# A ninth tile off ScalarE in six row pairs, and the second pair's x queued earlier, in a striped-window attention kernel

## The chip, the cores and the metric

The kernel runs on one core of one Trainium2 chip. The metric is the device time of one execution in microseconds. A measurement of a kernel is the median of several executions; one further execution is taken with the profiler on, and its trace gives the durations.

## The reference

The input x is one image of 224 × 224 positions with 96 channels, in bf16. Queries, keys and values come from one projection. The first 48 channels attend within horizontal stripes of 8 rows, the other 48 within vertical stripes of 8 columns; each stripe has 8 × 224 = 1792 tokens, and there are 28 stripes of each kind. The two halves are joined and projected.

```python
qkv = jnp.einsum('bhwc,cd->bhwd', x, wqkv)
q, k, v = (qkv[..., :C].copy(), qkv[..., C:2 * C].copy(), qkv[..., 2 * C:].copy())
scale = C2 ** (-0.5)
qh = q[..., :C2].reshape(B * nh, sw * W, C2)
...
ah = _softmax(jnp.einsum('bqc,bkc->bqk', qh, kh) * scale, axis=-1)
oh = jnp.einsum('bqk,bkc->bqc', ah, vh).reshape(B, H, W, C2)
...
av = _softmax(jnp.einsum('bqc,bkc->bqk', qv, kv) * scale, axis=-1)
ov = jnp.einsum('bqk,bkc->bqc', av, vv).reshape(B, nw, H, sw, C2)
...
return jnp.einsum('bhwc,cd->bhwd', o, wo)
```

## The kernel before

**Tiles.** The work goes by 28 pairs of stripes: P = 0 to 13 are the row pairs (horizontal stripes), P = 14 to 27 the column pairs. The two stripes of a pair lie in the two halves of the partitions. The 1792 queries of a pair are cut into four chunks of 512, 512, 512 and 256 columns, its keys into 14 tiles of 128. A tile, as the text uses the word, is one key tile against one chunk of queries for both stripes: 128 × 1024 scores (in the last chunk, two key tiles share one). A pair has 14 + 14 + 14 + 7 = 49 tiles.

**Three ways to the exponential.** Most tiles (kind A, letter `q` in the orders below) are scored by TensorE into one of two sets of PSUM banks (`qk_fn`, L642) and exponentiated by ScalarE (`emit_qk`, L812). The others avoid ScalarE: they are scored twice into banks of a ring of four (`s_fn`, L655), and VectorE and GpSimd work out the exponential by a polynomial in 16-bit numbers. Letter `1` is the first scoring, from which VectorE makes `qb` in two halves ("p1", L852). In kind P, GpSimd then runs three operations on the whole tile (L864, L867, L868). In kind R, VectorE makes a second step from the same banks ("p2", L854, two halves) and GpSimd only squares (L866). Letter `2` is the second scoring, from whose banks VectorE finishes the tile in two halves ("f", L857). `KINDS` (L22) says which of a chunk's last tiles are off ScalarE, chunk by chunk: `"PPR PPR PP "` means three, three, two and none, so eight in a pair (six P, two R) and 41 on ScalarE. `KIND_OF` (L44) picks an entry of `KINDS` for each pair; all have the same one.

**The rest of the work.** Letter `v` multiplies a finished tile with the values (`emit_pv`, L668) into an accumulating bank, which VectorE copies out at the end of a chunk (L829). Letter `k` is a fill for the next pair: its keys, a small correction by the mean key (a product of four columns, L492), its queries and values (L465, L510), each evicted by VectorE. Letter `f` is a fill that projects a finished part of the output with wo (L546 in the row stage, L582 in the column stage), again with its eviction by VectorE (L553 and L561; L589 and L594).

**The order.** The program of each engine is written out by a planner in the kernel's own Python code. `ORDER` (L45) has a string for each pair that says in which order TensorE issues its work; a loop over its letters calls `do_q`, `do_s`, `do_v` and `do_fill`. Assumed durations decide in which order VectorE and GpSimd take what becomes ready, and which bank is used. The eleven tiles after the first are scored twice over (`NTWICE`). `x_t`, fed by `XR1` and `XR2`, is the planner's assumption of when a pair's x is in place; it holds nothing back on the chip, where semaphores do.

**x on its way.** For row pairs from the second on, SP's queue, which is in order, moves x in steps: `block_x(P)` copies two stripes inside DRAM to another layout, `load_x(P)` loads them to `x_sb`, and `turn_x(P)` transposes them by DMA into `xT_sb[P % 2]`, from which the fills read. `keep_x(P)` stores the transposed x to DRAM for the column stage. At the program's start the queue holds pair 0's x, wqkv, block_x(1), block_x(2), and then the eight issues that bring wo and a one into `woh` and `wov`. Those wait for GpSimd to have cleared `woh` and `wov`. Behind them come load_x(1) and turn_x(1), then what `queue_prep` adds at the first tile of each pair:

```python
if P == 1:
    keep_x(0)
    load_x(2)
    keep_x(1)
    block_x(3)
elif P == 2:
    turn_x(2)
    load_x(3)
    keep_x(2)
    block_x(4)
```

Of the kernel before, what the change touches and what calls it, by code (L numbers as in the profile page):

```python
# [42 lines left out]

KIND_OF = [0, 0, 0, 0, 0, 0, 0, 0, 0, 0, 0, 0, 0, 0, 0, 0, 0, 0, 0, 0, 0, 0, 0, 0, 0, 0, 0, 0]  # L44
ORDER = [  # L45
    "kqkkqkq11qkqqk1qqkqvkqq1vvq1qkvq2vqvkvq1qvvvqkq2qvq2vqkvkqkqv1qkq1kqvvvq2vqv2qvvqkq1vvqkq2vqvkvq1qvvvqvkqkfqvvkqv",
    "2qvvq2vqvv1qvvqvvqvvq1vqvvfqv2qvkqkqvvkqkfqvvq2vqv1qvvq2kq2qvvq1vqvvqvvqkvvqkq1vvq2qkvqfvqv2qkvvqkq1vqfvqv2qkvqvvvq1qv1qvkvq",
    "fqvvfqvq2vqv1qvvvqvvqv1qvvq1qq2vqv1qvvqvvqv2qvvkqv1qkvqvq2vqkvkvqv2qvvvq1qvkfqvkqvkqv2qvvqvkq2vqvffqvqvkqvkkqkfqvvq1vqv2qvvvq1",
    "vqv2qvvqf1qvqvvvqvvq1fqqv1qvvq2vqv1qvvqkvqvfqkvqvkvq2qvq2vfqvvqkvq1kq2fqkqvvvq1qkvvqkq2vfqvvq2vqv2qkqvvkq1qvvvqv1qvqkvvkqff",
    "qvv2qvq1qvfqvvvqvq2vqvvvq2vq1qvqvvq1vqvkqv2qvvvqvkq1vqvfqvvqfvqvvvq1vqkkqvvq2kqv2qvvq2vqfvqkvq2vqvkq1qkvvqvkq1qvkvqvfqkvkvq",  # L50
    "fq1vvqv2qvvq1vqvvqvvvq1qvfqv2qvvq1vqvkq1qvvqvvkqkvq2qvvq1vvqkvq2qkfqvvkq1qvvq2qkvqfkqvvqf2qvvqv2qvvvqkq2vvqvkqfqvffqkvvqvvqk",
    "1qvvqv1qvvvq2qvv1qvvqvqv1qvvvqv1qvvq2vqv1qqvvvq2qfvqvvkq2vqvfqvvq1vqkvqvkq2vqvkvq1kq2qvkqkvvq2qvkvq1qvvvq1qkkqkvqv2qkq1q",
    "vvvqvq2vvq1qvvfqvfqvvvqfvq2vqv1qvvq2vqvkvq1qvvqvvvq2vqkvqkvkqv2qvfqkq1vqkvvq1qkvqvv2qkqkvqv1qvvvq2fqvvvqfvq2vqfvqkfqvvqkvq1vqkvvq2v",
    "qv1qvvvqfvqvvq2qvvvq1qv1qvvqvfqvv2qkvqvfqvkqvkq2vqvvkqf1qvvqvvqvqk1qvkqvvq2vqv2qvkqv1qkvqv2qkqvvqvv1qkqvvqv1qvvkqvfqvkvq2qvv2",
    "qvqvvfqvv1qqfvvqvvqv1qvq2vqkq1qkvvq2qvvqkvvq2fqvvqkvq1vqvkqvvqv2qvvqkvq1vqkvqkqvkq2vvqv2qvvq1vqvkqv1qkvqkqfvq1vvqv2qvvq",
    "2fqvqv1qvvvqvvqvvqf1qvvqv2qvvq1kqvqkvqkvq2qkvvfq1qvvvqfvqkqv2qkvqkvq1vqv1qkqvvfqfqvvfqkfqvvq2vqv2qvvq2vqkvqvvq1vvqkvq1vqvvqk",
    "2qvvq2vqfvq1qvvfqvvqvvq2vqvq2vqvv1qvq1vqv1qvvqkvvqkvqkvqvkq1vvq2qfvqkvq2fqvvfqvvq2vqvkqkvqvkq1vqv2qkvqvkq1vqkvqvqv1qfvvqvvkq2",
    "vq1qvqvvq2qvvffqvvq1qvvvqkvvq2qvv2qvqvvkq2vqv1qvkqvffqkvqvq1vkqvvqkvq1vq2qvvvqvfqkvvq2qvvvq1vqkvq2vqvkq2qvkqkvvvq1qkvvvqffqvvkvqf",
    "2qvvqv1qvvfqvvq1qvvvqfvqvvq1q2qvqkv1qvkq2qvvq1vqvkqqvvqvv2qvfqkqvk1q2qvvq2qfvqvkvq2qkvvq1qvv1qkqkvvq1qvkkqvvvq1qkvvvqvvq2v",
    "qvfqvv2qvfqvvq1vqvvq1vqv2qvvqvkq1vqvkvqvvqvkqkvfqv2qvvq2vqvvq2vqvfqkvq1vqkvqvkq2vqvkq1qvv2qvkqvkq1qvvvq1kqvvkqvfqv2qvvq2vqv1qv",  # L60
    "vqfvvqfvqvq1vvqfvqv2qvvqv2qkvqv2qvkqkqvkvq1kq1qvvqkvvqvq1fqvvqvkqvkqkq1vvqkqkv1qvfqq2vvqvq2vqv2qvvvq1vqvvq2vqkvfqvvqffqvvvqv",
    "vq2fqvvvqvqvfqvvv1qvvqqv1qfqvvq2vvqq1vvq2qkvkqkqv2qkvvq1qkvvqvvq2qvvq1fqvvkqvqkvq1vfqvvq2vqkqvv2qvqkkqv2qvvvvq2qvvvkq1qkvvq1vf",
    "qvvfqvvq1qvvvqvvfqvqvkq1qvvvqvkq2qfvvqvq2vvq2qvkvq1qvvvq2vvq1qkvqvkfqqvv2qvvkqq1vvq2qkvvq1qvkfqvkqvvqfqv2vqkvq1vq1qkvqv2qk",
    "vq1qvvvqvvq1qffqvvvqvvqvvq2vq1qvq2vqvkvq1fqvvqvvqv2qvqvkkqvvq1vqvfqkvvqv1qkqfvq2vqvvkqkq2vqvkq2qvkkqvvq2qvv1qvkqvvq1fqvvqk",
    "vfqvv2qvq1qfvqvvqvvqv2qvvqvvkq1qkkqvkqv1qfvqvfqkvq2qvq1vqvvvqv2qvq1vqv1qvvqv2qvvq2vfqvkqvvq2vqvkq1vqkkqvvq2vqkfqkvvqv1qvkvq",
    "2qvvq1vvqvvqvvq1fqvvvqv1qvvqv2qkkqfqvvqfvkqvvq1qkvqvkqv2qvq2vqv1qvkqvvq2vqkvqkq1vqfkqvvvq2qfvvqv2qvvq1vqvvq2vqvkvq2qkvvq1qvvk",
    "fqv2qvq1qvvqvvvq2qvvvq1fqvqfvvqvvqv1qkvqv2qvvqfq2vqvkqkvfqvkqvvq2vqvkq1qkvvqvqv1qvvq1vqkfqkvqfvqkvqkvq2vqkvqvvq1vqv2qvfqk",
    "vvvq1qfvqvvq2vvq2qvv1qvqvvqvvq1vvqkq2vqvv1qvvq2vq1qfqvvvqvkqvkqvkvqv1qkqkq1kq2qvvvq1qkqvv2qkvqfkqkvqvq2vvqv2qvkvqvq1vvq2qv",
    "v1qfqvvvqvvq1vqvfqvvq2vqvvvq1vqv2qvvkqq1vvqvkqvvvq1vqkfqvkqvv2qvvq2qvkvq2qkqk2qvvfqkvqfqvvfqvvvqv1qvkqvfqv1qvvqkvvqkfqvkvvq2qvvvq",
    "2vqvv1qfvqvvvqvq1vvqvvqv1qvq2qkvqkvqfvqv2qvvq1vqv2qvvkqkvfqvqkvq1vqvkqvvqv1qfqv2qvqv1qvq2vfqvvq2vqkqkvvqv1qvq2vqkkvq1qvkqvkv",  # L70
    "q2fqvvvqv1qqvvfqvqvvvq1qvvvq1vqkvqkq1vvqvqvv2qkqkvvq2vqv2qvq1vvqfqk2qvvqkqkkvq2qvvfqvvvq2qvv1qfqvkvqvvq2qvkvvq1qvvvkq1qfvvqfvk",
    "qvfqvq2vvq1qvqvvvq1qvvvqfvq2qvvvq1qvvkqkvq2vqv2qvfqkvqkvvq2vvqvvq2qv1qfqvvvqkqv1qvfqvvvq2qvkqkq1vkqkqvq2vfqvvvq1qvvkvq1qkvk",
    "q2qfvqvq1vqvvvqvqv1qfqvv1qvvqv2qfvvqvq2vvqv2qvq1fqvvqvvvq1vqvqfvvqvv2qfqvvvq2vqfvvq2qvv1qvfqvvfqvvfqv2qvvqffvfqvvq2vqvfqvvvqvqfffvvvvvvfff",
]
# [1126 lines left out]
```

## Time and profile before

| | us |
|---|---|
| median of 3 runs | 1083.1 (1077.69 to 1087.49) |
| profiled execution, its own time | 1083.81 |
| its span, first to last instruction | 1082.0 |
| busy: ScalarE | 1062.8 (98%) |
| busy: TensorE | 1050.6 (97%) |
| busy: VectorE | 1021.5 (94%) |
| busy: GpSimd | 956.4 (88%) |
| mean granted TensorE clock | 0.991 |

The lines of the profile name the engines by short names: PE is TensorE's matmuls and PEld its weight loads, ACT is ScalarE, DVE is VectorE, POOL is GpSimd, SPq is the queue of DMA issues on SyncE. Every row of a group gives the line of the kernel, the engine and operation, the written and read tiles with their shapes, the count, then the busy time and the mean duration of one, and last the idle time of the engine just before these instructions and what ended it. Operations of one engine overlap at their ends, so a mean duration can be longer than the pace. TensorE's busy time says little by itself, since the ends of matmuls are modelled. In a table of stretches each engine has its busy time and, in brackets, its instructions; PEclk is the granted TensorE clock as a share of full speed, and the last two columns are the mean busy share of the DMA engines and the GB/s moved.

### The profile page before, as it was taken

To read this page: it belongs to the slowest core of one execution; us is meant where nothing else is said; L and a number is where in the kernel's file an instruction comes from. 1 tells how busy PE (TensorE), PEld (TensorE's weight loads), DVE (VectorE), ACT (ScalarE), POOL (GpSimd) and SP (SyncE) were. 2 spreads that over 40 slices of the span, in tenths; PEclk is the share of its full clock that TensorE was granted. 3 is DMA by queue.
4 is the path that set the end of the run, shared out by engine and by line. 5 is a ranking of instruction groups with operands and counts; after the bars stand their busy time and mean duration, and the time that the engine had idled before them with its cause. 6 is when DMAs were issued, how large, how long until landed. Compare 5 with 4: busy or idle time off the path is not lost. (4 is left out here: it accounts for less than half of the span.)

```text
span 1082.0 us, 34436 instructions
## 1 busy us (share of the span) xinstructions
PE 1050.6 (97%) x14096; PEld 403.5 (37%) x14096; DVE 1021.5 (94%) x2246; ACT 1062.8 (98%) x1159; POOL 956.4 (88%) x597
## 2 busy tenths in 40 slices
PE   8999999999999999999999999999999999999997
PEld 3333433433333333334333333333433333333333
DVE  7799999999989999999999999999999999999998
ACT  7899999999999999999999999999999999999997
POOL 8979898879998888898999978998997997998895
PEclk9799999999999999999999999999999999999999
DMA  7997426516724650400001022112111110210112
GB/s 147 154 165 112 69 46 112 80 38 108 112 44 71 112 86 2 61 28 27 2 27 32 16 54 48 40 23 50 40 25 43 44 42 18 53 44 18 26 23 39
DMA packets 236994, 61.73 MB, mean 57 GB/s; under 512 B 227780, under 2 KB 234148, under 8 KB 236836
## 3 DMA queue, kind: packets, MB, share of 16 engines
q1 hardware_dynamic: 235716, 59.04, 30.1%
q8 instruction: 110, 1.80, 0.7%
q10 hardware_dynamic: 1120, 0.49, 0.2%
q14 instruction: 48, 0.39, 0.1%
HBM read 28.31 MB, written 28.21 MB: 52 GB/s over the span
## 5 line engine op out<-in xcount | busy, mean ns | idle before, releaser
L812 ACT ACTIVATE PT<-ps 128x1024 bf16<-128x1024 f32 x1148 | 1058.5, 1081 | 9.5 <-PE ps L642 8.2
L642 PE MATMUL ps<-QT_sb,KT_sb 49*64 49x512 bf16 (+1 forms) x5420 | 480.0, 364 | 15.3 <-ACT PT L812 9.7
L668 PE MATMUL ps<-PT,V_sb 128*49 128x512 bf16 (+1 forms) x3136 | 466.3, 364 | 0.1
L864 POOL TENSOR_TENSOR PT<-qb 128x1024 f16<-128x1024 f16 x168 | 316.8, 1894 | 68.1 <-DVE qb L852 45.0
L868 POOL TENSOR_TENSOR PT<-PT,qb 128x1024 f16<-128x1024 f16 x168 | 355.8, 2127 | 8.5
L857 DVE SCALAR_TENSOR_TENSOR PT<-ps,PT 128x512 uint16<-128x512 f32 x448 | 290.5, 683 | 22.7 <-PE ps L655 13.3
L852 DVE TENSOR_SCALAR qb<-ps 128x512 f16<-128x512 int16 x448 | 291.6, 683 | 10.5 <-PE ps L655 7.3
L642 PEld LDWEIGHTS ps<-QT_sb,KT_sb 49*64 49x64 bf16 x5420 | 144.0, 104 | 295.3 <-ACT PT L812 274.1
L668 PEld LDWEIGHTS ps<-PT,V_sb 128*49 128x49 bf16 x3136 | 133.7, 103 | 211.9 <-issue 171.7
L867 POOL TENSOR_SCALAR PT<-PT 128x1024 f16<-128x1024 f16 x168 | 175.8, 1046 | 14.2
L655 PE MATMUL ps<-QT_sb,KT_sb 50*64 50x512 bf16 (+2 forms) x1792 | 180.1, 392 | 5.1 <-DVE PT L857 1.8
L866 POOL TENSOR_TENSOR PT<-PT 128x1024 f16<-128x1024 f16 x56 | 106.1, 1894 | 19.9 <-DVE PT L854 16.1
L594 DVE SCALAR_TENSOR_TENSOR out_all<-ps,rc,Ph_sb 128x96 bf16<-128x96 f32 x392 | 96.9, 307 | 0.6
L655 PEld LDWEIGHTS ps<-QT_sb,KT_sb 50*64 50x64 bf16 (+2 forms) x1792 | 51.2, 104 | 64.8 <-DVE PT L857 18.7
L854 DVE SCALAR_TENSOR_TENSOR PT<-ps,qb 128x512 f16<-128x512 int16 x112 | 72.3, 681 | 0.0
L829 DVE CAST OT_sb<-ps 113x512 bf16<-113x512 f32 x112 | 69.1, 617 | 3.2 <-PE ps L668 2.5
L470 DVE TENSOR_SCALAR_CACHE_REDUCE KT_sb<-ps 128x512 bf16<-128x512 f32 x108 | 64.9, 618 | 4.4 <-PE ps L465 3.8
L479 DVE CAST QT_sb<-ps 128x512 bf16<-128x512 f32 (+1 forms) x111 | 67.4, 614 | 1.2 <-PE ps L465 1.0
L517 DVE CAST V_sb<-ps 128x480 bf16<-128x480 f32 (+1 forms) x84 | 51.5, 620 | 4.3 <-PE ps L510 3.7
L561 DVE TENSOR_TENSOR Ph_sb<-ps,rc 128x480 bf16<-128x480 f32 (+1 forms) x84 | 52.0, 620 | 1.9
L465 PE MATMUL ps<-xT_sb,w_sb 97*64 97x512 bf16 x224 | 41.5, 371 | 2.0 <-DMA xT_sb<-out_all 1.9
L465 PE MATMUL ps<-xT_sb,wq_sb 97*64 97x512 bf16 x224 | 41.3, 368 | 0.1
(60 smaller groups left out, 309.2 us busy)
## 6 DMA issues: line engine op xcount, KB each, us to landing
...
xT_sb<-out_all SPq DMA_TRANSPOSE x26, 4.8
...
```

Source lines behind the costliest of these rows:

```text
L465: ins = e.matmul(bk[64 * w:64 * w + 64, 0:qs], lhsT=lw, rhs=xT_sb[b][0:C + 1, w, q0:q0 + qs], start=True, stop=True)
L594: return e.scalar_tensor_tensor(out_sb[b][:, w, kt, :], bk3[:, s, 0:C], rc[ri][:, s:s + 1], Ph_sb[:, kt, j, :], ALU.mult, ALU.add)
L642: ins = e.matmul(bank(SETS[s] + w)[64 * kh:64 * kh + 64, i * t["qs"]:(i + 1) * t["qs"]], lhsT=KT_sb[b][64 * w:64 * w + CA, kt * 128 + 64 * ...
L655: ins = e.matmul(bank(bp[w])[64 * kh:64 * kh + 64, 0:512], lhsT=KT_sb[b][64 * w:64 * w + nr, kt * 128 + 64 * kh:kt * 128 + 64 * kh + 64], ...
L668: ins = e.matmul(bank(pb)[64 * w:64 * w + CA, 0:t["qs"]], lhsT=V_sb[b][:, w, kt, :], rhs=PT[slot][:, ca:ca + t["qs"]], start=st and i == 0 ...
L812: S.commit("act", 0.0, D_ACT, None, lambda e, s=s, slot=slot: e.activation(PT[slot][:], ps[:, 512 * SETS[s]:512 * SETS[s] + 1024], ACTF.Ex ...
L852: fn, reads, writes = lambda e: e.tensor_scalar(q, low16(bi), m, a, ALU.mult, ALU.add), bk, qk
L857: fn, reads, writes = lambda e: e.scalar_tensor_tensor(y.bitcast(U16), bank(bi), 128.0, y.bitcast(FP16), ALU.mult, ALU.add), bk + ptk, ptk
L864: sq = lambda e: e.tensor_tensor(y, q, q, ALU.mult)
L866: return [("pool", D_SQ, lambda e: e.tensor_tensor(y, y, y, ALU.mult), yk + ["pser"], yk)]
L867: af = lambda e: e.tensor_scalar(y, y, PB, 128.0 * PA, ALU.add, ALU.mult)
L868: ml = lambda e: e.tensor_tensor(y, y, q, ALU.mult)
```

## The change

A second entry of `KINDS` has an R tile more, in the third chunk, so nine tiles of a pair are off ScalarE and 40 are on it. Pairs 2, 4, 6, 8, 10 and 12 use it. Load_x(1) and turn_x(1) move up to directly behind block_x(1), ahead of wo's eight issues, and block_x(2) moves behind those. Turn_x(2) is no longer called in `queue_prep` but when the last query fill of pair 0 is planned. `x_t` takes a fixed time for pair 2. All strings of `ORDER` but one (pair 20's) are new; only the first is shown here. In all strings together there are 1142 letters `q` for 1148, and 230 each of `1` and `2` for 224.

```diff
-KINDS = ["PPR PPR PP "]
+KINDS = ["PPR PPR PP ", "PPR PPR PPR "]
 KINDS = [k.split(" ") for k in KINDS]
...
-XR1, XR2 = 19.0, 5.0
+XR1, XR2 = 19.5, 43.0
...
-KIND_OF = [0, 0, 0, 0, 0, 0, 0, 0, 0, 0, 0, 0, 0, 0, 0, 0, 0, 0, 0, 0, 0, 0, 0, 0, 0, 0, 0, 0]
+KIND_OF = [0, 0, 1, 0, 1, 0, 1, 0, 1, 0, 1, 0, 1, 0, 0, 0, 0, 0, 0, 0, 0, 0, 0, 0, 0, 0, 0, 0]
 ORDER = [
-    "kqkkqkq11qkqqk1qqkqvkqq1vvq1qkvq2vqvkvq1qvvvqkq2qvq2vqkvkqkqv1qkq1kqvvvq2vqv2qvvqkq1vvqkq2vqvkvq1qvvvqvkqkfqvvkqv",
+    "kqkqkkq1qkqk1q1qqqvvkqkq1vkqq2vkqvvkq1qkq1qvvqvvq2vq2qvkqvkqv1qkvqv1qvkvqv2qvvq2vqvkqkq1vqv2qkvqkvkqvqvv1qkvvq2qvv",
...
         block_x(1)
-        block_x(2)
+        load_x(1)
+        turn_x(1)
         flags = set()
         for (dst, r0) in ((woh, 0), (wov, C2)):
...
                 dma("sp", ["one", "woz"], ["wo"], dst[p0:p0 + 1, C:C + 1], one_sb[0:1, 0:1], "w1", 128)
+        block_x(2)
...
         spin(S.done[("dve", S.cnt["dve"] - 1)], 128)
-        load_x(1)
-        turn_x(1)
...
             elif P == 2:
-                turn_x(2)
                 load_x(3)
...
-        x_t = {0: 7.4, 1: XR1}
+        x_t = {0: 7.4, 1: XR1, 2: XR2}
...
                 if P + 1 < NP:
-                    if P > 0:
-                        x_t[P + 1] = st + XR2 if P == 1 else 0.0
                     queue_prep(P + 1)
...
-                r = x_t[P]
+                r = x_t.get(P, 0.0)
...
             emit_fill(f, b[0])
+            if g == ("Q", 0, NCH - 1):
+                turn_x(2)
```

More of the change, by code (lines that the diff above doesn't have):

```diff
@@ new lines @@
+    "kqkqkkq1qkqk1q1qqqvvkqkq1vkqq2vkqvvkq1qkq1qvvqvvq2vq2qvkqvkqv1qkvqv1qvkvqv2qvvq2vqvkqkq1vqv2qvkqkvkqvqvv1qkvvq2qvv",
+    "2qvvqvfq1vqvvqvvqvfqvvq1vqv2qvvqvkq1vqv2qvkqkvvq2vqv1qvvqvkqvvq1vqkq2vqvkqkffqvfqvvqkq1vqkvq2kqvvq2vqv2qvvvq1qvvkqfvqvkvq1qv",
+    "2qvvq1vvqvqvvvq1q1q1qvvvqvvqvfqvvqkvq2vfqkvqkvq1qkvvq2vqv1qvvq2kq2qkvqvvvq2vqkqkq1vkqvvqkvqvffqvvq2qvvfqv2qvvq1qkfqvvqkvvf",
+    "q2vqvvfqv2qvvq1qvv1qvvqvvqvvq1vfqvvq1qvvq1vqvvvqv2qvvq2qvkvq2qvkvqkfqkvqvvq1kq2qvvkqkvq2fqvvvq1qvvkq2qvv1qvvqfkqvvkq2qvvkfqvkq",
@@ new lines @@
+    "v2qvvq1fqvvvq2vfqvvqvq1fqvvvqvvqv2q1qvvvq2qvkvq1qvv1qvqvvvqkkqkvvvq2qkvv1qkqvkqkq1vvq2qkvqfkvqv2qkvq1qvqvkqvvvfq1qvvvq1vqv2qv",
+    "vq2vqfvvq2qvv1qvvqvvqvq1vqv1qq2vvq1qkvqvvqfvqvkqv2qfqkvqv2qkvvvq1fqvqvv2qkqvfqv1qvvvfq2qvvkqv2qkqkvqv2qkvqvkvvqfqvvkvq2vqv1qvkv",
+    "q1qvvq1vvqvvqv1qvqvv1qvvfqv2vqq1vvqvvq2qvqkkvvq2qkvvvq1qkvvq1vqvkq2qkkqkkq2qvvkqq2vvv1qqkvvvqvfqkvvq1vq1qvvq2qvvq1fqvvqvv",
+    "vqfvq2vqv2qvvq1vqvvq1vqv2qvvq1vvqkqvvkqvvvq1qvv2qvvq2vqkvkqvfqfkqvvq2vqkfqvvq2vqv1qvvq2vfqvkqkqvkq1vfqvvq2qvkqvvvq1vqkvq2vqvfqkvv",
@@ new lines @@
+    "fq1qvfqvvvqvvqv2qvvfqv1qvqv2qvkvqkvq1qv2qvkqkvvfq1qvvvqvvq1qvkvq2qvkvq2qvq2vqvkq1vqv1qvvvqvqkkqkvq2vqv1qvvqfvvq1qvv2qvkqk",
+    "vq1qvvqvvq2vq2qvvvqv1qvvqvvkq2qkvvqv2qvvvq1qvvkkqvq1vqkvqvvvqf1qvvvqvkfqfvqvkq2qvv1qvvqf2qvqv2qkqvkvq1qvvkqv2qkqvvkvq2qvvvvq1fqvvv",
+    "qv1qvqvvvqv2qfqvvq2kq1qvvvq2qvfqvv1qfqvkvqkq1vvqvqfvkqvvqf2qkqvv1qfvqv2qkqkqkvq1vvq2qkvqkvq1vvqvvqv2qvvvq2qvkvqv1qvfqk",
+    "vvfqv2qvvq1vfqqvvv2qvvq1vqvqvkq1qfvqvvkq1qkvvq1qkvvqkqv2qvvq2vqvfqvvq1vqfvkqkqkfqkvqfkqvvq2vqv1qvvq2vqv2qvkvqkqv1q1qvvqv2qv",
@@ new lines @@
+    "fvqvv2qvq1qvvvqvqvfqvvvq1vqvkq2qfvqkvqv2qvvq1vq2qfqkvvkqvvq1vqqvvkvq1qvkvqkkqv1qkvqkfqkvqvv2qvvq2vqv2qvq1vqv1qvvvvq2qkvvq2vvfqf",
+    "qvvfqvvvqvq1qvvvqvvq1qvvqk2q2qvvvq1qv2qfqvkqvvqvkq2vvq1qkvqvkqvvkq1qkqfvqvkfqvvqv2qvvq1vvq2qkvqkvq1vvqvq2vvqkfqvvvq1qvv2qk",
+    "vvq1qvvvfqvqvvqfvvqvvvqv1qvqkq1vq2qvvq2vq1qvvqvkvqkq2qfvqkvvqvvq2kq1qkkqkfqvqv2qvvqkfqvv1qvqvkvq2qvv2qvkqvvq1vqvkqfvvq1vq",
+    "fvvq2qvvvqv1qvvfqvqvvvqv2qvvqvkq1qkkqvkqv1qfvqvfqkvq2qvvq1vqvvvqv2qvq1vq1qvvqv2qvvq2vfqvkqvvq2vqvkq1vqkkqvvq2vqkfqkvqvv1qvkvq",
```

37 lines of the change are left out of this document (11 added, 26 removed).

## The prediction

> **What bounds the kernel now.** I began with the page: the share of each engine, then the costliest groups.
>
> ```profile
> span 1082.0 us, 34436 instructions
> ...
> L812 ACT ACTIVATE PT<-ps 128x1024 bf16<-128x1024 f32 x1148 | 1058.5, 1081 | 9.5 <-PE ps L642 8.2
> ...
> L857 DVE SCALAR_TENSOR_TENSOR PT<-ps,PT 128x512 uint16<-128x512 f32 x448 | 290.5, 683 | 22.7 <-PE ps L655 13.3
> L852 DVE TENSOR_SCALAR qb<-ps 128x512 f16<-128x512 int16 x448 | 291.6, 683 | 10.5 <-PE ps L655 7.3
> ...
> L866 POOL TENSOR_TENSOR PT<-PT 128x1024 f16<-128x1024 f16 x56 | 106.1, 1894 | 19.9 <-DVE PT L854 16.1
> ...
> L854 DVE SCALAR_TENSOR_TENSOR PT<-ps,qb 128x512 f16<-128x512 int16 x112 | 72.3, 681 | 0.0
> ```
>
> ScalarE's exponentials fill 1058.5 of 1082.0 us, and only 9.5 us of idle time stand before them. They overlap (1081 ns each), so their pace is 1058.5 / 1148 = 0.922 us a tile. Next came the table of stretches, to see where ScalarE is not full.
>
> ```profile
> core 0: us, PE busy (x) PEld busy (x) DVE busy (x) ACT busy (x) POOL busy (x), PEclk, DMA share, GB/s
> ...
> 20.00:30.00 10.00, 7.23 (x70) 2.19 (x68) 7.69 (x16) 8.46 (x10) 9.84 (x7) 0.90 1.01 150
> 30.00:40.00 10.00, 10.00 (x64) 2.62 (x62) 6.69 (x15) 6.42 (x8) 9.26 (x6) 0.50 1.10 151
> 40.00:50.00 10.00, 9.98 (x160) 3.79 (x156) 8.56 (x14) 9.41 (x11) 9.06 (x7) 0.92 0.85 145
> ...
> 1000.00:1050.00 50.00, 48.34 (x648) 18.75 (x642) 49.79 (x126) 49.95 (x55) 44.26 (x28) 1.00 0.13 24
> ...
> 84.00:500.00 416.00, 407.25 (x5476) 156.18 (x5474) 386.38 (x748) 414.05 (x452) 374.28 (x221) 1.00 0.42 70
> 236.00:312.00 76.00, 73.92 (x982) 27.97 (x984) 70.14 (x135) 74.23 (x81) 68.97 (x42) 0.98 0.49 80
> 600.00:1050.00 450.00, 440.51 (x5972) 169.79 (x5968) 442.63 (x1075) 449.57 (x489) 400.75 (x238) 1.00 0.16 36
> ```
>
> From 600 to 1050 us (column pairs) ScalarE works 449.57 of 450 us: it is the bound, with VectorE right behind at 442.63 (98.4%). In the row stage, 84 to 500 us, VectorE is at 386.38 of 416 (92.9%), and ScalarE loses 1.95 us, nearly all (76 − 74.23 = 1.77) in 236 to 312. The hole is at the start: between 20 and 50 us ScalarE lacks 1.54 + 3.58 + 0.59 = 5.71 us, at a TensorE clock that falls to 0.50. The timeline shows what stands before both clock drops (start, duration, engine and line; in brackets the idle time before and what ended it).
>
> ```profile
> 2.12 3.56 SPq L281 DMA_DIRECT2D xp_dram<-in_x_dram  x4
> ...
> 8.34 3.01 ACT L812 ACTIVATE PT<-ps 128x1024 bf16<-128x1024 f32 x3 [0.97 <-PE ps L642]
> ...
> 10.41 1.02 SPq L281 DMA_DIRECT2D woh<-in_wo_dram  x2
> ...
> 14.95 1.22 SPq L281 DMA_DIRECT2D out_all<-xp_dram  x2
> ...
> 20.45 0.41 PE L642 MATMUL ps<-QT_sb,KT_sb 49*64 49x512 bf16 x4 [0.24 <-ACT PT L812]
> ...
> 22.14 1.53 SPq L393 DMA_TRANSPOSE xT_sb<-out_all  x1
> ...
> 24.30 0.41 PE L642 MATMUL ps<-QT_sb,KT_sb 49*64 49x512 bf16 x4
> ...
> 26.63 0.41 PE L465 MATMUL ps<-xT_sb,w_sb 97*64 97x512 bf16 x2 [1.93 <-DMA xT_sb<-out_all]
> ...
> 27.43 2.85 ACT L812 ACTIVATE PT<-ps 128x1024 bf16<-128x1024 f32 x3 [1.54 <-PE ps L642]
> ...
> 298.98 0.53 PE L492 MATMUL ps<-ksum,wqT 128*64 128x4 bf16 x4 [0.74 <-DVE PT L857]
> ```
>
> The clock beside them, in stretches of 2 us:
>
> ```profile
> 28.00:30.00 2.00, 1.64 (x12) 0.31 (x10) 1.38 (x3) 2.00 (x3) 1.92 (x2) 0.50 0.89 129
> ...
> 302.00:304.00 2.00, 2.00 (x36) 0.94 (x34) 1.46 (x3) 1.34 (x2) 1.99 (x2) 0.50 0.00 0
> ```
>
> SP's queue is in order. Pair 1's load (14.95) stands behind the eight issues for wo (from 10.41 on), its second transpose goes out at 22.14, and TensorE, which asks for that x after its 18th tile (24.30), stands still for 1.93 us until 26.63. From 28 us the clock is 0.50; its mean of 0.92 over 40 to 50 says that it rises at 41.6. The other drop, at 302, follows a gap of 0.74 us before a fill of four columns.
>
> **The change, part by part.**
>
> *Six activations fewer.* Six row pairs give a ninth tile away: 6 × 0.922 = −5.53 us, if ScalarE stays the bound. Cross-check: with 1142 activations and no idle time the span would be 8.34 + 1142 × 0.922 + tail. The tail comes from this row, where ScalarE ends 0.39 us into the last 7, so 6.61 us:
>
> ```profile
> 1075.00:1082.00 7.00, 1.29 (x24) 0.54 (x20) 2.92 (x14) 0.39 (x1) 0.00 (x0) 0.81 0.30 56
> ```
>
> That is 1067.9 us, and 1069.7 with the 1.81 us between the profiled run's time (1083.81) and its span. Less is hardly to be had.
>
> *What the six tiles cost elsewhere.* All are of kind R: two p1, two p2 and two last steps on VectorE, one square on GpSimd, two score passes on TensorE for one taken away. VectorE: 2 × (291.6/448 + 72.3/112 + 290.5/448) = 3.89 us each. A row pair now takes 386.38 / (452/41) = 35.05 us of VectorE; a nine-tile pair 38.94 in 40 × 0.922 = 36.88 us: 106%. Nine- and eight-tile pairs alternate: 73.99 us in 74.68, or 99.1%. The column stage holds 98.4% with a full ScalarE, and 1000 to 1050 holds 49.79/50 = 99.6%. If 98.4% were the most, the six double pairs would take 6 × 73.99 / 0.984 = 451 us and not 448, +3; if 99.6% goes, nothing. I take +1.0, nearer to the second. Below nothing is excluded, as it is added work. GpSimd: 106.1/56 = 1.89 us, so (2 × 374.28/11.02 + 1.89) / 74.68 = 93%: covered by the 10% that it idles now.
>
> *TensorE.* The timeline shows the cost of a change between row-tiled work (L642, L655) and full-height work (L668), and a row of the waits who waits for whom:
>
> ```profile
> 53.87 0.41 PE L642 MATMUL ps<-QT_sb,KT_sb 49*64 49x512 bf16 x4
> 54.11 0.39 PE L655 MATMUL ps<-QT_sb,KT_sb 52*64 52x512 bf16 x4
> 54.43 0.40 PE L668 MATMUL ps<-PT,V_sb 128*49 128x512 bf16 x2
> ```
>
> ```profile
> PEld ps L642 <- ACT PT L812: 274.1, 779, 0.8
> ```
>
> 0.24 us from start to start without a change, 0.32 with one. Counted over the order strings there are 1947 changes before and 1901 after: −46 × 0.08 = −3.7 us, against six passes more, +6 × 0.24 = +1.4. Net −2 us, on an engine whose weight loads wait 274 us for ScalarE: nothing on the path. If it were on the path, a gain of up to 2.
>
> *Pair 1's x ahead of wo.* Block_x(1), load_x(1) and turn_x(1) now stand in SP's queue before wo's eight issues and block_x(2). From the load's issue to the data took 26.63 − 14.95 = 11.68 us. The load must now wait for block_x(1) to land. The copies of both pairs, issued from 2.12 on, ended by:
>
> ```profile
> 9.00:10.00 1.00, 1.00 (x36) 0.65 (x32) 1.00 (x4) 1.00 (x2) 0.70 (x6) 1.00 0.25 78
> ...
> 15.00:16.00 1.00, 0.97 (x14) 0.25 (x10) 1.00 (x3) 1.00 (x2) 0.92 (x2) 1.00 0.00 0
> ```
>
> All four by some 9.3 us (busy for 0.25 of that stretch). Pair 1's two are the first in the queue: at an even rate they end half-way between 2.12 and 9.3, at 5.7. So the load issues between 5.7 and 9.3 and x is there at 17.4 to 21.0; as pair 0's own x goes ahead of the copies I take 8, so 19.7. The new order asks for it after the 14th tile, whose scores were issued at 20.45, so at about 20.8: a stall of 0.2 us at worst, and the spell in which the DMA engines idle now (0.00 at 15 us) is used. If the stall goes and the clock drop with it, 5.71 us come back; I leave 0.5 for what is late next (the same engines then carry pair 0's stores): −5.2. Bounds: 0 and −5.7.
>
> *What is moved back.* Wo's eight issues (14.95 − 10.41 = 4.5 us) and block_x(2) now follow turn_x(1). These rows show their users:
>
> ```profile
> 28.49 2.59 SPq L281 DMA_DIRECT2D out_all<-xp_dram  x2
> ...
> 40.42 7.62 SPq L393 DMA_TRANSPOSE xT_sb<-out_all  x2
> ...
> 50.88 0.32 PE L546 MATMUL ps<-woh,OT_sb 49*64 49x97 bf16 x6
> ```
>
> Wo is first read at 50.88: some 28 us of cover. Block_x(2) then goes out near 22 and is read by the load that stood at 28.49. Turn_x(2) is called elsewhere in the program, but between the same neighbours of SP's queue, so it stays near 40.4 to 48.0 and lands by 53 (the one of 22.14 took 4.5 to 26.63); its first reader comes after the 52nd tile, 8.34 + 51 × 0.922 = 55.4 or later. Cost 0; with that cover gone, a second stall like the first. The constants XR1 and XR2 only feed the program's own planning. The other orders are new but for one line: the drop at 302 (1.77 us) may vanish or come elsewhere, so I count 0 within ±1.8.
>
> **Sum** against the profiled execution: 1083.81 − 5.53 − 5.2 + 1.0 = 1074.1. That run is 0.7 above the median of 1083.1, so I forecast 1073.4.
>
> **A rule that speaks against it.** TensorE stood still for 1.93 us and 0.74 us ahead of the two drops. The Trainium skill ("TensorE: Matmul & The Clock Gate", Part 1 and the closing table) says that the clock is halved after an idle window of about 3.4 us, and asks only that no gap be longer than some 3 us. By that rule the 1.93 us gap is not the cause, the drop would come back, and the time would be that of the first rival; the trace speaks rather against it, since both drops come within 3 us of a gap that is too short for it.
>
> **The rivals.**
> 1. *The drop is not the stall's doing.* Only ScalarE's 1.54 us at 27.43 come back: 1083.81 − 5.53 − 1.54 + 1.0 − 0.7 = 1077.0. For: TensorE is still thinly fed at the start, and the drop outlasts the gap by 13 us. Against: it begins 1.4 us after the gap. 0.15.
> 2. *The change doesn't do what it says*: x lands after 22 and the stall stays, as the new order asks 3.9 us earlier. 1083.81 − 5.53 + 1.0 − 0.7 = 1078.6. For: the upper bound, 21.0, has no slack. Against: the DMA engines idle at 15 us. 0.14.
> 3. *Slower: VectorE becomes the bound in the nine-tile pairs.* 38.94 us of work in 36.88: if the order cannot pass the surplus to the next pair, TensorE waits for PSUM banks, 2.06 us a pair, and each such wait halves the clock as at 302 (1.77): 1073.4 − 1.0 + 6 × 3.83 = 1095.4. It cancels the gain from 1.8 us a pair on. For: a gap of 0.74 us was enough. Against: 99.6% beside a full ScalarE at 1000 to 1050. 0.13.
> 4. *Better:* no drop in the row stage and no cost of density: 1073.4 − 1.77 − 1.0 = 1070.6. 0.13.
>
> **How the numbers follow.** The forecast has 0.45, at 1071 to 1076. Against 1083.1, 1% (about what a measurement of this kernel can tell from no change) lies at 1072.3. Faster: rival 4 and half of the forecast, 0.36. Slower, over 1094: most of rival 3, 0.10. The rest, 0.54, is within 1%. The range runs from 1069 (the floor of 1069.7, less the 0.7) to 1084: it takes in rivals 1 and 2 and the mild half of rival 3, and leaves out the rest of that and a little of each side. The likeliest case's own range is 1071 to 1076.
>
> **What would show it.** 1142 activations and 62 squares at L866; ScalarE's busy time near 1053. TensorE's wait at L465 for the DMA gone, clock 1.00 from 20 to 50 us, ScalarE above 29 of those 30. VectorE at 99% from 84 to 500 us with ScalarE losing under 3 us there. I am wrong if the clock still halves near 28 us (rival 1 if there was no wait before it, rival 2 if there was), or if TensorE's waits for VectorE at L655 grow by several us in the nine-tile pairs.

## The result, and the profile after

| | before | after |
|---|---|---|
| median | 1083.61 us of 12 runs (1077.69 to 1094.74) | 1075.12 us of 12 runs (1074.39 to 1076.25) |
| profiled execution, span | 1083.81 us, 1082.0 | 1074.76 us, 1073.0 |
| mean granted TensorE clock | 0.991 | 0.999 |

The ratio of the times is 0.9915, with a 95% interval of 0.989 to 0.9941: some 8.5 us faster, which is less than 1% (the interval reaches just over it). The executions of the kernel before differ by the clock they were granted: of 82 that stand beside the experiments below, 28 had a mean clock of 0.997 to 1.000 (median 1077.7 us), 15 one of 0.991 to 0.994 (1082.7) and 39 one of 0.980 to 0.988 (1088.7), whereas all 12 executions after had 0.998 to 1.000. The profile of before, at 0.991, is one of the middle group. The costliest groups on the page of the kernel after (line, engine, operation, tiles, count, busy us, mean ns of one, idle time before them and what ended it):

```profile
span 1073.0 us, 34516 instructions
...
PE 1045.8 (97%) x14120; PEld 407.0 (38%) x14120; DVE 1038.4 (97%) x2282; ACT 1058.9 (99%) x1153; POOL 967.0 (90%) x603
...
L811 ACT ACTIVATE PT<-ps 128x1024 bf16<-128x1024 f32 x1142 | 1054.6, 1073 | 4.4 <-PE ps L644 3.0
...
L865 POOL TENSOR_TENSOR PT<-PT 128x1024 f16<-128x1024 f16 x62 | 117.5, 1896 | 16.0 <-DVE PT L853 9.5
```

There are 1142 activations and 62 squares, and ScalarE's idle time ahead of the activations has gone from 9.5 to 4.4 us. (Lines 642, 655, 668, 465, 812, 852, 854 and 857 of before are 644, 657, 670, 467, 811, 851, 853 and 856 here.) The same stretches as before the change:

```profile
20.00:30.00 10.00, 9.37 (x94) 2.81 (x90) 9.93 (x20) 10.00 (x12) 9.76 (x7) 1.00 0.75 147
30.00:40.00 10.00, 9.94 (x136) 3.99 (x134) 8.94 (x19) 9.95 (x12) 9.92 (x6) 1.00 1.06 159
40.00:50.00 10.00, 10.00 (x154) 3.81 (x154) 9.15 (x17) 10.00 (x12) 9.76 (x7) 1.00 0.76 147
...
84.00:500.00 416.00, 407.42 (x5546) 158.90 (x5544) 405.10 (x789) 413.81 (x448) 384.11 (x227) 1.00 0.43 72
```

The hole at the start is filled: ScalarE works 29.95 of the 30 us from 20 to 50, at a full clock. In the row stage VectorE has gone from 386.38 to 405.10 us, and ScalarE loses 2.19 us there, about as before. The timeline shows why the start is full:

```profile
6.37 1.60 SPq L281 DMA_DIRECT2D out_all<-xp_dram  x2
10.30 4.80 SPq L393 DMA_TRANSPOSE xT_sb<-out_all  x2
15.15 1.57 SPq L281 DMA_DIRECT2D woh<-in_wo_dram  x2
...
20.24 1.73 SPq L281 DMA_DIRECT2D xp_dram<-in_x_dram  x2
...
21.71 0.39 PE L467 MATMUL ps<-xT_sb,w_sb 97*64 97x512 bf16 x2
```

Pair 1's load goes out at 6.37 (before: 14.95), its transposes at 10.30, and the first fill that reads pair 1's x starts at 21.71 with no wait in brackets.

**Reading lateness instead of idle time.** A busy share hides part of what ScalarE loses. An activation lasts longer than the pace (1.07 us against 0.92), so one that starts late by up to some 0.15 us still overlaps the one before it and leaves no gap. I therefore took the start of the n-th activation from the timeline of each run, less the start of the first, less (n − 1) × 0.9205 us, and call this its lateness. 0.9205 is the pace of undisturbed stretches. The table has the runs up to new_columns, each by its one profiled execution (us; the last column is the start of the first activation, then that of the last); what is read of the others stands with them.

| tile | 82 | 164 | 287 | 328 | 492 | 533 | 616 | last | starts |
|---|---|---|---|---|---|---|---|---|---|
| before | 7.39 | 7.60 | 7.47 | 9.48 | 8.90 | 9.29 | 9.21 | 10.11 | 8.34, 1074.27 |
| after | 0.70 | 1.09 | 3.08 | 3.20 | 3.80 | 5.23 | 5.45 | 6.67 | 8.86, 1065.82 |
| queue_only | 0.59 | 0.77 | 0.73 | 1.43 | 0.98 | 1.25 | 1.17 | 1.96 | 8.84, 1066.61 |
| busy_gap | 2.04 | 2.19 | 2.19 | 4.28 | 3.81 | 4.20 | 4.12 | 4.99 | 10.05, 1070.85 |
| no_ninth | 0.74 | 1.05 | 2.81 | 2.75 | 3.39 | 5.06 | 5.17 | 6.88 | 9.22, 1071.91 |
| late_x | 6.65 | 7.02 | 9.07 | 9.06 | 9.98 | 11.32 | 11.65 | 12.99 | 8.69, 1071.97 |
| old_around | 0.55 | 1.13 | 3.35 | 3.45 | 4.21 | 5.56 | 5.66 | 6.78 | 9.03, 1066.10 |
| new_columns | 0.74 | 0.93 | 0.86 | 1.42 | 0.95 | 1.30 | 1.16 | 3.76 | 8.87, 1068.44 |

Before and after differ so: up to tile 82, −6.69; from there to 287, +2.30; from 287 to 328 (the clock drop at 302 us), −1.89; from 328 to 616, +2.52; in the column stage, +0.32. That is −3.44. With six activations fewer (−5.52), a first activation 0.52 us later and a tail 0.55 us shorter (1082.0 − 1074.27 = 7.73, now 7.18) it makes the 9.0 us by which the span is shorter. So two large gains are there, and in the two other stretches of the row stage the new orders gave back 4.8 us.

### The profile page after: what moved, and what is told of

It is laid out like the page before. It is cut to its first block, busy times and chain, and to the rows that moved or that the text cites. A ratio compares the mean times of both kernels' runs of the same rounds, so it can differ in the third digit from the quotient of the medians.

```text
span 1073.0 us, 34516 instructions
## 1 busy us (share of the span) xinstructions
PE 1045.8 (97%) x14120; PEld 407.0 (38%) x14120; DVE 1038.4 (97%) x2282; ACT 1058.9 (99%) x1153; POOL 967.0 (90%) x603
## 4 chain that ended last, share of the span: by engine, by line
PE 48%; ACT 28%; DVE 12%; issue 7%; POOL 3%; DMA 0%; ACTq 0%; DVEq 0%; POOLq 0%
ACT PT L811 28%; PE ps L670 17%; PE ps L644 17%; PE ps L657 6%; DVE PT L856 4%; DVE qb L851 3%; PE ps L467 3%; DVE out_all L596 2%; PE ps L512 2%; POOL PT L863 2%; DVE PT L853 1%; PE ps L548 1%; POOL PT L867 1%; DVE OT_sb L828 1%; PE ps L584 1%
## 5 line engine op out<-in xcount | busy, mean ns | idle before, releaser
L670 PE MATMUL ps<-PT,V_sb 128*49 128x512 bf16 (+1 forms) x3136 | 460.0, 362 | 0.5 <-DVE PT L856 0.3
L856 DVE SCALAR_TENSOR_TENSOR PT<-ps,PT 128x512 uint16<-128x512 f32 x460 | 299.3, 683 | 10.5 <-PE ps L657 4.3
L851 DVE TENSOR_SCALAR qb<-ps 128x512 f16<-128x512 int16 x460 | 298.8, 682 | 8.4 <-PE ps L657 5.9
L657 PE MATMUL ps<-QT_sb,KT_sb 50*64 50x512 bf16 (+2 forms) x1840 | 184.6, 390 | 6.7 <-DVE PT L856 1.0
L865 POOL TENSOR_TENSOR PT<-PT 128x1024 f16<-128x1024 f16 x62 | 117.5, 1896 | 16.0 <-DVE PT L853 9.5
L853 DVE SCALAR_TENSOR_TENSOR PT<-ps,qb 128x512 f16<-128x512 int16 x124 | 80.7, 680 | 0.0
L472 DVE TENSOR_SCALAR_CACHE_REDUCE KT_sb<-ps 128x512 bf16<-128x512 f32 x108 | 65.2, 616 | 0.8 <-PE ps L467 0.4
```

The source lines that it names most:

```text
L657: ins = e.matmul(bank(bp[w])[64 * kh:64 * kh + 64, 0:512], lhsT=KT_sb[b][64 * w:64 * w + nr, kt * 128 + 64 * kh:kt * 128 + 64 * kh + 64], ...
L670: ins = e.matmul(bank(pb)[64 * w:64 * w + CA, 0:t["qs"]], lhsT=V_sb[b][:, w, kt, :], rhs=PT[slot][:, ca:ca + t["qs"]], start=st and i == 0 ...
L851: fn, reads, writes = lambda e: e.tensor_scalar(q, low16(bi), m, a, ALU.mult, ALU.add), bk, qk
L856: fn, reads, writes = lambda e: e.scalar_tensor_tensor(y.bitcast(U16), bank(bi), 128.0, y.bitcast(FP16), ALU.mult, ALU.add), bk + ptk, ptk
L865: return [("pool", D_SQ, lambda e: e.tensor_tensor(y, y, y, ALU.mult), yk + ["pser"], yk)]
```

## The experiments

All ran in four sets, each beside the kernel before on one chip, the sets on different chips. The median of the kernel before went from 1083.06 to 1088.25 us from one set to the next, as the mix of these groups changed, so the intervals of the ratios are wide, and differences below are read from the kernels' medians and the lateness. A difference under 1 us between kernels of different sets says little by itself; the lowest time of the kernel before lay between 1076.68 and 1077.34 us in the four sets.

**queue_only: the kernel before with the move in SP's queue alone.**

```diff
...
         block_x(1)
-        block_x(2)
+        load_x(1)
+        turn_x(1)
...
+        block_x(2)
...
-        load_x(1)
-        turn_x(1)
```

> The kernel before with nothing changed but SP's queue: load_x(1) and turn_x(1) directly behind block_x(1), block_x(2) behind wo's issues; orders and kinds as before. Theory (the wait for x makes the clock drop): no wait of TensorE for the DMA near 25 us, clock 1.00 from 20 to 50 us, ScalarE above 29 of those 30 us, and 5.7 us less than before: about 1078. Rival (the drop comes from something else): the wait is gone, the clock still halves near 28 us, and only the 1.5 us of ScalarE's wait come back: about 1082.

Measured: 1075.9 us (1075.22 to 1081.25), ratio 0.9953 (0.9921 to 0.9986), lower than both expectations. Its stretches:

```profile
20.00:30.00 10.00, 9.16 (x92) 2.90 (x88) 9.51 (x20) 10.00 (x12) 9.84 (x7) 1.00 0.71 144
30.00:40.00 10.00, 9.93 (x136) 3.93 (x136) 9.64 (x19) 10.00 (x12) 9.92 (x6) 1.00 1.09 159
40.00:50.00 10.00, 9.96 (x152) 3.67 (x152) 8.85 (x17) 10.00 (x12) 9.76 (x7) 1.00 0.74 144
...
294.00:296.00 2.00, 2.00 (x24) 0.62 (x22) 2.00 (x5) 1.85 (x3) 2.00 (x2) 1.00 0.00 0
296.00:298.00 2.00, 2.00 (x38) 0.88 (x38) 2.00 (x4) 2.00 (x3) 1.91 (x2) 1.00 0.00 0
```

ScalarE is full from 20 to 50 us, and the drop near 300 us is gone too, though the orders are the old ones. The gap of TensorE that stood ahead of it has kept its place in the program and its length (the row of before had 0.74 us):

```profile
292.74 0.53 PE L494 MATMUL ps<-ksum,wqT 128*64 128x4 bf16 x4 [0.74 <-DVE PT L857]
```

So the queue's move alone brings this kernel within 1 us of the whole change, and a part of that is a drop that it doesn't touch. Of its ten executions nine had a clock of 0.997 to 1.000, and one, of 1081.25 us, 0.992. Against the executions of before that kept the clock (1077.7) the move gives 1.8 us, about the 1.54 us that ScalarE waits for x: so most of the 7 to 8 us between the medians is the half clock.

**busy_gap: the kernel before with work in TensorE's gap.** Nine products of a constant tile stand ahead of pair 1's first fill, in the bank that the fill then overwrites.

```diff
...
+            if f["gives"] == ("K", 1, 0):
+                def busy_pe(e, bk=bank(bi)):
+                    for _ in range(9):
+                        ins = e.matmul(bk[0:64, 0:512], lhsT=warm[:, 0:64], rhs=warm[:, 0:512], start=True, stop=True)
+                    return ins
+                S.commit("pe", 0.0, 1.95, 2.15, busy_pe, ["warm"], [("bank", bi)], fresh=[("bank", bi)])
```

> The kernel before with nine matmuls of 512 zero columns (1.9 us) put into the wait for pair 1's x: the data comes as late as before and ScalarE waits as before, but TensorE is busy meanwhile. Theory (TensorE's idleness is what halves the clock): clock 1.00 from 28 to 42 us, ScalarE loses 1.5 us and not 5.7 between 20 and 50, time about 1079.4. Rival (lateness of x or the DMA load does it, not the idle engine): the clock halves all the same, time as before, 1083.6.

Measured: 1080.01 us (1077.08 to 1084.57), ratio 0.9988 (0.9955 to 1.0021).

```profile
26.15 1.70 PE L810 MATMUL ps<-warm 128*64 128x512 bf16 x7
27.66 0.40 PE L465 MATMUL ps<-xT_sb,w_sb 97*64 97x512 bf16 x1
...
20.00:30.00 10.00, 9.13 (x95) 3.33 (x93) 8.26 (x17) 8.41 (x10) 9.92 (x6) 1.00 1.04 151
30.00:40.00 10.00, 9.87 (x116) 3.60 (x116) 9.54 (x20) 10.00 (x12) 9.84 (x7) 1.00 1.13 158
...
296.00:298.00 2.00, 2.00 (x15) 0.45 (x14) 1.83 (x6) 1.02 (x1) 2.00 (x2) 0.52 0.00 0
```

x comes about as late as before (the fill that reads it starts at 27.66, 17.6 us after the first activation; before, 18.3) and ScalarE still loses 1.59 us in the first stretch, but the clock stays at 1.00 and nothing more is lost: 2.04 us at tile 82 for 7.39. The drop near 296 us is still there; tiles 287 to 328 lose 2.09 us. One profile could be luck, since before kept a full clock in 28 of 82 executions too. The ten executions say more: seven had 0.996 or more, three 0.992 or 0.993, and none was as low as the 39 of before at 0.988 or less. So TensorE's idle time is what brings the long spells of half clock on; where the drops of those three lay was not profiled.

**late_x: the kernel after with SP's queue as before** (the diff of queue_only, reversed).

> The changed kernel with SP's queue as before, so that pair 1's x comes at about 26.6 us while the order asks for it at about 21. Theory: TensorE stands still for over 5 us, the clock halves afterwards for some windows; 5 us for the wait and about 4 for the clock: about 1084. Rival (the drop at 28 us has another cause): the wait alone, about 1080, with the clock at 1.00.

Measured: 1082.07 us (1080.8 to 1082.53), ratio 0.9991 (0.9961 to 1.0021).

```profile
26.04 0.64 PE L465 MATMUL ps<-xT_sb,w_sb 97*64 97x512 bf16 x2 [4.34 <-DMA xT_sb<-out_all]
```

```profile
20.00:30.00 10.00, 5.50 (x44) 1.51 (x40) 4.77 (x12) 5.17 (x6) 7.20 (x5) 0.78 1.03 151
30.00:40.00 10.00, 9.80 (x94) 2.97 (x90) 8.55 (x18) 9.29 (x11) 9.76 (x7) 0.88 1.21 166
```

The new first order asks for x earlier, so the wait grows from 1.93 to 4.34 us; the half clock that follows is shorter, and the lateness at tile 82 is 6.65 instead of 7.39. All ten executions had a clock of 0.994 to 0.996: after this longer wait none kept the full clock. The result lies between the two expectations. Against the kernel after it says once more what the move is worth: 1082.07 − 1075.12 = 6.95 us.

**no_ninth: the kernel after with the six ninth tiles on ScalarE again.** The strings stay as they are, but for the two letters of the ninth tile.

```diff
...
+        if c == "1":
+            n1 += 1
+            if n1 in ends:
+                seq[i] = "q"
+        elif c == "2":
+            n2 += 1
+            if n2 in ends:
+                seq[i] = ""
...
+KIND_OF = [0] * 28
```

> The changed kernel with the six ninth tiles given back to ScalarE: in its orders the first scoring of each becomes a letter q in its place, the second falls away. Queue and other orders as changed. In the changed kernel the tiles 12 to 506 come every 0.929 us, where the kernel before had 0.921 in undisturbed stretches. Theory (the density of VectorE's work in the row stage made ScalarE slower): the pace goes back to 0.921, so the six tiles were worth only 1.6 us net: about 1076.8. Rival A (the six tiles are worth their full 5.5 us and the pace is that of the new orders): the pace stays at 0.929, about 1080.6.

Measured: 1081.61 us (1080.52 to 1085.56), ratio 0.9991 (0.9959 to 1.0024); 6.5 us slower than the kernel after. Seven of the ten executions had a clock of 0.997 or less; the three others took 1080.5 to 1080.9, which is 5.4 to 5.8 us slower. The rival was right, and VectorE's density as the cause fell. The tiles are worth their full 5.5 us: the lateness of the last activation is about the same (6.88 and 6.67). And the 4.4 us that the row stage loses (0.74 to 5.17 from tile 82 to 616; after: 4.75) are lost without a ninth tile as well, at a VectorE that has room on the whole:

```profile
84.00:500.00 416.00, 402.66 (x5462) 156.44 (x5454) 381.55 (x747) 413.92 (x448) 370.35 (x219) 1.00 0.41 70
```

**old_around and new_columns: the new strings in parts.** old_around is the kernel after with the old strings at the start (up to pair 2) and from pair 15 on; new_columns is queue_only with the new strings from pair 15 on. In the diff, before and after are all strings of a kernel joined; the planner takes one long string as well.

```diff
-ORDER = [after]
+ORDER = [before[:238] + after[238:1863] + before[1857:]]
...
-ORDER = [before]
+ORDER = [before[:1857] + after[1863:]]
```

> The changed kernel with the old orders on both sides: the start up to pair 2 (tiles 1 to 82) and from pair 15 on as in the kernel before; only the row pairs 2 to 14, with their six ninth tiles, keep the new orders. Counted by tiles of ScalarE, the changed kernel falls behind the kernel with only the queue moved by 0.8 us before its 12th tile, 2.7 us in the rows and 1.2 us in the columns. Theory (the new strings themselves cost this, each where it stands): start and columns come back, about 1073.1, the fastest so far. Rival (the orders are equally good and the slower pace follows from the ninth tiles or is noise): 1075 as the changed kernel.

> The kernel with only the queue moved (old orders, no ninth tile, 1075.9), but with the new strings from pair 15 on. Theory (the new column strings are slower by themselves): 1.2 us more, about 1077. Rival: 1075.9, as the queue-only kernel.

Measured: old_around 1074.84 us in 4 runs (1074.73 to 1075.26), ratio 0.9894 (0.9859 to 0.9928), the same as the kernel after, which is the rival's number; its reason, the ninth tiles or noise, doesn't fit no_ninth. New_columns took 1077.42 in 5 runs (1076.87 to 1077.99), ratio 0.9922 (0.9892 to 0.9952), 1.5 us slower than queue_only. Its last activation is 1.8 us later than queue_only's, and 1.2 of that arises from tile 616 to 625, right behind the seam between the old strings and the new, where ScalarE has one gap of 0.74 us. Neither the new start nor the new columns give anything; the row strings keep their 5.11 us of lateness (0.55 to 5.66) in old_around.

**load_queue and load_after: more work for VectorE.** Twenty-four copies of an accumulator into a tile that nobody reads, in pairs 2 to 13, on queue_only and on the kernel after.

```diff
...
+            if 2 <= P <= 13 and c < 2:
+                S.commit("dve", 0.0, 0.6, 0.75, lambda e: e.tensor_copy(dum[0:64 + CA, 0:qs], bank(pb)[0:64 + CA, 0:qs]),
+                         [("bank", pb)], [("dum",)])
```

> The same 24 copies in the kernel with only the queue moved: VectorE's share in the rows goes from 93% to 96%, near the changed kernel's 97%, with the old orders and no ninth tile. If the density of VectorE's work as such slows ScalarE: 2 to 3 us more, 1078 to 1079. If it is the orders: 1076, as without the copies.

> The changed kernel with 24 copies more on VectorE in the row pairs 2 to 13 (the output of the first two chunks of each pair is copied out twice, 0.62 us each): 15 us of work, where VectorE idles 12.3 us between 84 and 534. Theory (the row stage stands at VectorE's bound): 1079 or more. Rival (there is room left and what slows the rows is the order): under 1 us, 1076.

Measured: 1085.3 us (1084.63 to 1086.55) and 1085.18 (1084.41 to 1086.49), ratios 1.0008 (0.9977 to 1.004) and 0.9999 (0.9972 to 1.0025): 9.4 and 10.1 us more than without the copies. Load_queue came out far over all that was expected of it. Load_after fits its theory's "1079 or more", but since load_queue loses as much, that doesn't show the changed kernel's rows to be at VectorE's bound. The copies take 16.4 us in load_queue,

```profile
L833 DVE CAST dum<-ps 113x512 bf16<-113x512 f32 x24 | 16.4, 681 | 0.0
```

and by tile 616 ScalarE is 8.7 us later than in queue_only. Yet VectorE idles 24 us of the row stage there:

```profile
84.00:500.00 416.00, 402.40 (x5398) 153.46 (x5396) 391.74 (x759) 411.54 (x445) 368.93 (x218) 1.00 0.42 70
```

Room in VectorE's busy share is thus not room for work that the order wasn't made for. A copy also holds its accumulator's bank longer: in load_queue TensorE's weight loads wait 10.0 us in all for the copies, half of it at the value products. How much of the loss is that, and how much VectorE's time, the runs don't part.

**Where the row strings lose.** After, the largest of ScalarE's visible gaps in the row stage lie in pair 6, in the rows below, and in pair 12 (0.30 us at 468.71):

```profile
244.09 18.02 ACT L811 ACTIVATE PT<-ps 128x1024 bf16<-128x1024 f32 x19 [0.38 <-PE ps L644]
262.49 1.94 ACT L811 ACTIVATE PT<-ps 128x1024 bf16<-128x1024 f32 x2 [0.38 <-PE ps L644]
```

Ahead of the first, TensorE's timeline reads:

```profile
242.56 0.41 PE L670 MATMUL ps<-PT,V_sb 128*49 128x256 bf16 x4
242.90 0.41 PE L657 MATMUL ps<-QT_sb,KT_sb 52*64 52x512 bf16 x4
243.24 0.40 PE L670 MATMUL ps<-PT,V_sb 128*49 128x256 bf16 x4
243.57 0.63 PE L644 MATMUL ps<-QT_sb,KT_sb 49*64 49x512 bf16 x8
```

A finishing score pass and two value products stand ahead of the scores that ScalarE waits for. **q_early1** and **q_early2** move six such letters of pairs 6 and 12 ahead by one and by two places. The string of pair 6 in q_early2:

```diff
-    "q1qvvq1vvqvvqv1qvqvv1qvvfqv2vqq1vvqvvq2qvqkkvvq2qkvvvq1qkvvq1vqvkq2qkkqkkq2qvvkqq2vvv1qqkvvvqvfqkvvq1vq1qvvq2qvvq1fqvvqvv",
+    "q1qvvq1vvqvvqv1qvqvv1qvvfqvq2vq1vvqvvq2qqvkkvvq2qkvvvq1qkvvq1vqvkq2qkkqkkq2qvvkqq2vvqv1qkvvvqvfqkvvq1vq1qvvq2qvvq1fqvvqvv",
```

> Theory (the new row strings put two to four value products or a score pass for VectorE ahead of a score pass that ScalarE already needs, and TensorE, in order, issues it too late): with six such letters q of pairs 6 and 12 moved one place earlier, the lateness of ScalarE that the changed kernel gains between tiles 246 and 287 (1.3 us) and between 492 and 533 (1.4 us) shrinks by half, and the time is near 1074. Rival (TensorE has not the time in these pairs, so the wait only goes to another tile): both steps stay and the time is 1075 to 1076.

> The same six letters moved two places earlier. Theory: both steps go nearly whole, 1072.5. Rival: the steps stay in size and move to the tiles behind, 1075 to 1077.

Measured: 1075.22 us (1074.68 to 1075.47), ratio 0.9917 (0.9879 to 0.9954), and 1075.91 (1075.46 to 1077.24), ratio 0.9912 (0.9877 to 0.9946). The rival was right: the gaps move to the tiles behind, and the lateness at tile 616 is 5.84 and 6.45 for 5.45. It isn't the place of these letters.

**less_pe and less_dve: half of TensorE's value products, or half of VectorE's half steps, left out in pairs 6 and 12.**

```diff
-                        ins = e.matmul(bank(pb)[64 * w:64 * w + CA, 0:t["qs"]], lhsT=V_sb[b][:, w, kt, :],
-                                       rhs=PT[slot][:, ca:ca + t["qs"]],
+                        n = t["qs"] // 2 if t["P"] in (6, 12) and not st else t["qs"]
+                        ins = e.matmul(bank(pb)[64 * w:64 * w + CA, 0:n], lhsT=V_sb[b][:, w, kt, :],
+                                       rhs=PT[slot][:, ca:ca + n],
...
-            bi, cols = tl["bp"][h], slice(512 * h, 512 * h + 512)
+            n = 256 if tl["P"] in (6, 12) else 512
+            bi, cols = tl["bp"][h], slice(512 * h, 512 * h + n)
...
```

> The changed kernel with half of TensorE's value products of pairs 6 and 12 left out (all but the first of a chunk stream half the columns; some 95 products a pair, about 0.1 us less each), orders and plans as they are. Theory A (TensorE itself is short in these two pairs): ScalarE's two steps of lateness there (1.3 and 1.4 us) go, and the time is near 1072.4. Theory B (TensorE stands in order behind score passes that wait for banks which VectorE frees late): both steps stay, 1075. Theory C (GpSimd, busy 39.1 of 40 us there, sets it): both stay, 1075.

> The changed kernel with half of VectorE's work on the tiles that it and GpSimd exponentiate in pairs 6 and 12 left out (256 of 512 columns in the two or three half steps of each tile), orders and plans as they are. Theory B: the two steps of lateness go, near 1072.4. Theory A and theory C: both stay, 1075.

Measured: 1074.23 us (1074.16 to 1074.82), ratio 0.9907 (0.9868 to 0.9946), and 1074.22 (1074.08 to 1085.17), ratio 0.9911 (0.9866 to 0.9957). The lateness gained in the two pairs (tiles 246 to 287, and 492 to 533) is 1.30 and 1.43 us after, 1.10 and 0.98 in less_pe, 0.71 and 0.90 in less_dve. So no theory holds alone: VectorE's half brings back 1.1 of 2.7 us, TensorE's 0.7. (Both came out 0.9 us under the kernel after, but in another set.) The stretch of pair 6, first after, then in less_dve:

```profile
242.00:264.00 22.00, 20.62 (x272) 7.88 (x270) 21.46 (x44) 21.05 (x23) 21.67 (x13) 1.00 0.47 81
```

```profile
242.00:264.00 22.00, 20.82 (x282) 7.98 (x278) 16.97 (x44) 21.45 (x24) 21.67 (x13) 1.00 0.48 83
```

GpSimd is busy 21.67 of 22 us in both, and VectorE 21.46 of 22 after: where the loss is, both are full, whatever the mean of the stage says. But full engines alone don't cost ScalarE anything. In queue_only they are nearly as full in this stretch, and ScalarE has no gap:

```profile
242.00:264.00 22.00, 21.43 (x264) 8.00 (x260) 21.30 (x43) 22.00 (x25) 21.59 (x14) 1.00 0.52 87
```

Less work for GpSimd was not tried. The rest of the loss in these two pairs stays open, and so do the 2 of the 4.75 us that lie in the other row pairs.

## Why the prediction was right, and where its terms were off

The forecast was 1073.4 us and the result 1075.12, inside the likeliest case's own range of 1071 to 1076. The total is better than its parts: two gains were larger than the sum had them (by 1.5 and 1.9 us), and a term that was put at nothing cost 4.8. That these nearly cancel is luck.

There is luck in the base too. The sum takes 5.2 us for pair 1's x off a profile whose clock had dropped, and the median of 1083.1 lay near that profile's time; but in 28 of the 82 executions of before there was hardly a drop. Against these (1077.7) the change gives 2.6 us. That fits an estimate from the rows: 5.5 for the activations and 1.5 for ScalarE's wait, less the 4.2 us by which the new strings lose more in the row stage than queue_only's (4.75 − 0.58). So most of the 8.5 us between the medians are spells of half clock that no longer come.

**Six activations, −5.53: right.** no_ninth puts them at 5.5 us by lateness, at 5.4 to 5.8 by its executions at full clock and at 6.5 by the medians.

**Pair 1's x, −5.2: right in mechanism, too small.** The wait and the half clock together cost 7.39 − 0.70 = 6.7 us in the profiled execution. The step that was mis-sized is the sum of ScalarE's missing busy time from 20 to 50 us, 5.71, and the 0.5 taken off it. Busy time doesn't show activations that start late but still overlap, so 1.0 us more was lost than it shows, and nothing came up in the place of the stall. The load left SP's queue at 6.37, inside the bounds of 5.7 and 9.3 and earlier than the 8 that was taken; x was asked for at 21.71 and was there.

**The stall as cause of the half clock (against rival 1): shown** by busy_gap, where x is as late and only TensorE's idle time is filled, and by the clocks of its ten executions. The stall needn't halve the clock every time, though: a third of the executions of before kept it, with the same queue; their stall was not profiled. (The drop ends 41.67 − 26.63 = 15 us after the gap, not 13 as rival 1 has it.) The Trainium skill ("TensorE: Matmul & The Clock Gate", Part 1 and the closing table) has the clock halve after an idle window of about 3.4 us and asks for no gap over some 3 us. The measurement here differs: 1.93 us were enough in the profiled execution, and the measurement decides.

**The drop at 302 us, 0 within ±1.8: the gain came (−1.89), as the prediction supposed it might.** Of the kernels with the old strings there and no copies added, all have the gap of 0.74 us in their profiles (0.74 in queue_only, 0.79 in busy_gap, 0.69 in new_columns); the kernel after, no_ninth and old_around, whose row strings are new, have none. After, the fill has no wait in brackets:

```profile
290.80 0.53 PE L494 MATMUL ps<-ksum,wqT 128*64 128x4 bf16 x4
```

But the gap doesn't always halve the clock: queue_only and new_columns have it and no drop. There tiles 287 to 328 lose 0.6 to 0.7 us, in before and busy_gap, with the drop, 2.0 to 2.1. So the new strings are worth some 0.6 us there in any case, and the other 1.3 only where the clock would have dropped.

**VectorE's density, +1.0: small, as taken, and the working holds.** The ninth tiles add 405.10 − 381.55 = 23.55 us to VectorE from 84 to 500 us, against 6 × 3.89 = 23.3 in the prediction; the share is 97.4% and not 99.1%, because with the new strings that stretch holds fewer tiles (448 activations for 452) and, without the ninth tiles, less work of VectorE (no_ninth 381.55 us, before 386.38). Their price is the difference between after and no_ninth in the row stage, 4.75 − 4.43 = 0.3 us. Rival 3, a VectorE that stops the row stage, did not come.

**The new orders, 0: this is the term that failed.** They cost 4.8 us against before outside the drop, and 4.2 in the whole row stage against queue_only; no_ninth shows that they do so without the ninth tile (4.43 − 0.58 = 3.9). The prediction read them only for the drop at 302 and for TensorE's mode changes. The last of its signs of being wrong came: the idle time ahead of TensorE's weight loads for the score passes, most of it ended by VectorE, rose from 64.8 us before (65.2 in queue_only) to these, after and in no_ninth:

```profile
L657 PEld LDWEIGHTS ps<-QT_sb,KT_sb 50*64 50x64 bf16 (+2 forms) x1840 | 52.5, 103 | 78.3 <-DVE PT L856 21.7 <-DVE qb L851 17.7 <-DVE KT_sb L472 5.3
```

```profile
L682 PEld LDWEIGHTS ps<-QT_sb,KT_sb 50*64 50x64 bf16 (+2 forms) x1792 | 51.2, 104 | 74.7 <-DVE PT L881 20.0 <-DVE qb L876 17.7 <-DVE KT_sb L497 5.6
```

Some 10 of the 13.5 us more belong to the strings, and most of the rise lies in the row stage (84 to 500 us: 22.1 in queue_only, 33.3 after, 29.9 in no_ninth). Why they lose is shown in part only, for pairs 6 and 12. Whether ninth tiles can be had with the old rows' lateness was not tried.

**Wo and block_x(2) moved back, 0: right.** Block_x(2) went out at 20.24, and no wait for wo or for pair 2's x appears among ScalarE's or TensorE's waits.
